# Another instruction list for the first three token blocks of a retention-and-MLP kernel, with named PSUM banks

## The chip, the cores and the metric

The kernel runs on one core of a Trainium2 chip. The metric is the device time of one execution in microseconds; of several runs the median is given. Five engines work side by side, each through its own queue in order: PE (matrix multiplications), DVE, ACT and POOL (element-wise work, copies, conversions) and SP, which here only issues DMAs. POOL and ACT issue some DMAs as well.

## The reference

Retention for 8 batches of 8 heads, 576 tokens and 64 channels, then one MLP with a sine activation over all 4608 tokens:

```python
scores = scale * q @ k.T                        # per batch and head, scale = 1/8
ret    = scores * gamma[h] ** (i - j)           # where i >= j, else 0
x      = (ret @ v) -> [4608 tokens, 512]        # heads side by side
h      = x @ w_in                               # 512 -> 2048
g      = h + sin(alpha * h) ** 2 / (alpha + 1e-9)
out    = g @ w_out                              # 2048 -> 512
```

gamma[h] is 1 - 2^(-5-h). Inputs and output are float32; the kernel multiplies in float16.

## The kernel before, in words

**Tokens.** The first 512 tokens of each batch make a block of the MLP: block n (0 to 7) needs batch n. The last 64 tokens of all eight batches, the ends, make block 8. A batch's 512 tokens are two halves, p = 0 and 1, of two chunks each.

**Retention of a batch** (class Attention). `load` brings q, k or v of a half from DRAM, 512 KB, by SP, into one of six `raw` buffers. `cast` multiplies q and k with the decay factors and makes float16 (v only becomes float16). `turn` transposes on PE and `take` copies the result from PSUM; for batches 2 and later `crossed` transposes by DMA instead, issued by SP. `scores` multiplies k and q (L318), `masked` applies the causal mask on DVE and gives `ret` (L329). `outer` makes each chunk's k-times-v state (L266), `evict`, `take_sum`, `more`, `next_sum` and `to_state` carry it from chunk to chunk (POOL or DVE). `values` multiplies ret and v in two passes (L356), `add_states` adds the earlier state times q (L374), and `keep` copies the result to xT (float16), the input of the MLP.

**MLP of a block.** There are 16 slices of 128 hidden channels, fc 0 to 15. `project(n, fc)` is four matmuls into one PSUM bank (L486), `sine` on ACT (L494), `square` on ACT, DVE or POOL (L503, L505), `product` on DVE gives gT (L510). `gemm2(n, u)` is four matmuls of the output (L530): output tile c = u // 4 (128 tokens), and slices 4 (u % 4) to 4 (u % 4) + 3. `finish` copies a tile to SBUF and stores it. A projection and a unit of gemm2 are the same amount of PE work, four matmuls of 512 columns.

**Weights.** `load_w_in(g)` brings the columns of fc 4g to 4g + 3, `load_w_out(g)` the rows of the same slices; POOL issues them, and the DMA converts them to float16. `wait_for_w_out(g)` is a small DMA on SP that reads that group, so that what stands behind it in SP's queue is issued only when the group has arrived.

**The order.** Everything stands in a manual schedule: each engine executes its instructions in the order of the program text, and waits for what an instruction reads and for the release of the buffer that it writes. From L571 to L1024 the order of batches 0 to 3 and blocks 0 to 2 is one list written out. From L1026 a loop over blocks 3 to 8 places the work of batch n + 1, the loads and casts of batch n + 2 and the ends between the projections of block n and the units of gemm2 of block n - 1. `keep_busy` multiplies zeros.

**PSUM.** Eight banks: tag `hp` has three buffers of one bank, `op` one, `mm` two of two banks. Whoever asks for a buffer of a tag gets the one that comes free first.

## Time and profile before

| what | us |
|---|---|
| median of 3 runs | 319.76 (319.76 to 322.72) |
| profiled execution | 320.69 |
| its span | 318.9 |
| PE busy in the span | 301.3 (94%) |
| DVE, ACT, POOL busy | 216.9, 174.0, 137.3 |
| first projection starts | 19.9 |
| loop starts (first projection of block 3) | 115.5 |
| last block's units of gemm2 begin | 299.4 |

Times in the profile are from the span's start. A busy PE is not PE at its peak, and idle time of an engine that ends no wait costs nothing. L numbers are lines of the kernel before. A row of the timeline gives start, duration, engine, line, operation, output<-inputs and count; what stands in brackets is the idle time before and what ended it.

### The profile page before, as it was taken

The numbers are of one execution on the slowest core, as the hardware profiler recorded it, in microseconds if no ns is written. First come the engines' busy times: TensorE is split into PE (matmuls) and PEld (weight loads), VectorE is DVE, ScalarE is ACT, GpSimd is POOL, SyncE is SP. The second block draws the span as 40 slices with busy tenths as digits, with TensorE's granted clock in tenths as the row PEclk, the third lists the DMA queues.
The fourth block names the chain that finished last, engine by engine and source line by source line (L and its number), as shares of the span: only waits on it lengthen the run. The fifth ranks groups of instructions, "written<-read, shape, count | busy, mean of one in ns | idle before, by whom it ended". The sixth has DMA issues, their size and how long they took to land.

```text
span 318.9 us, 7711 instructions
## 1 busy us (share of the span) xinstructions
PE 301.3 (94%) x3180; PEld 143.9 (45%) x3180; DVE 216.9 (68%) x316; ACT 174.0 (55%) x269; POOL 137.3 (43%) x140
## 2 busy tenths in 40 slices
PE   7889999699799999999999999999999999999994
PEld 2554454244344444444444444444444444444442
DVE  2778877669468989687878787878746565655500
ACT  3548654498356645464547454745465565456411
POOL 0866542472866961993299329922720000000000
PEclk9999999799999999999999999999999999999999
DMA  8999999999994559996999589952352111111232
GB/s 211 266 202 209 299 242 280 218 239 232 213 248 144 84 113 251 262 171 134 245 255 184 123 240 257 155 113 67 72 82 49 35 35 33 36 33 34 57 77 66
DMA packets 103108, 49.96 MB, mean 157 GB/s; under 512 B 44944, under 2 KB 98592, under 8 KB 103072
## 3 DMA queue, kind: packets, MB, share of 16 engines
q1 hardware_dynamic: 98352, 45.12, 63.1%
q0 software_dynamic: 4224, 4.19, 8.0%
q8 instruction: 25, 0.41, 0.6%
q10 hardware_dynamic: 496, 0.15, 0.2%
q14 instruction: 11, 0.09, 0.1%
HBM read 36.85 MB, written 9.44 MB: 145 GB/s over the span
## 4 chain that ended last, share of the span: by engine, by line
PE 78%; DMA 9%; DVE 6%; ACT 2%; POOL 2%; issue 2%; ACTq 0%; POOLq 0%; DVEq 0%
PE hps L486 35%; PE ops L530 34%; DMA v<-in_v_dram 5%; DMA q<-in_q_dram 3%; PE sc L318 2%; PE o L356 2%; DVE gT L510 2%; DVE ret L329 2%; DVE ss_t L505 1%; DMA k<-in_k_dram 1%; PE kv L266 1%; ACT s_t L494 1%; PE o L374 1%; PE idle L543 1%; ACT ss_t L503 1%
## 5 line engine op out<-in xcount | busy, mean ns | idle before, releaser
L494 ACT ACTIVATE s_t<-hps,alpha_t 128x512 f16<-128x512 f32 x144 | 97.9, 685 | 97.1 <-PE hps L486 96.7
L530 PE MATMUL ops<-w_out,gT 128*128 128x512 f16 x580 | 144.0, 378 | 0.9 <-ACT osb L102 0.5
L510 DVE SCALAR_TENSOR_TENSOR gT<-ss_t,inva,hps 128x512 f16<-128x512 f16 x144 | 106.1, 746 | 49.4 <-ACT ss_t L503 42.1
L486 PE MATMUL hps<-xT,w_in 128*128 128x512 f16 (+1 forms) x520 | 129.3, 380 | 3.6 <-DVE xT L104 2.1
L486 PEld LDWEIGHTS <-w_in 128*128 128x128 f16 x584 | 56.8, 98 | 71.2 <-issue 5.9
L530 PEld LDWEIGHTS <-gT 128*128 128x128 f16 x580 | 54.3, 98 | 64.5 <-DVE gT L510 0.9
L505 DVE TENSOR_TENSOR ss_t<-s_t 128x512 f16<-128x512 f16 x88 | 54.0, 614 | 17.3 <-ACT s_t L494 17.2
L329 DVE TENSOR_TENSOR ret<-sc,mask 128x1024 f16<-128x1024 f32 x32 | 38.6, 1218 | 1.7 <-PE sc L318 1.6
L293 POOL TENSOR_TENSOR s<-kvs,cn 128x256 f16<-128x256 f32 x20 | 13.4, 670 | 49.4 <-ACT kvs L102 47.1
L161 POOL TENSOR_TENSOR k<-k,cn 128x1024 f16<-128x1024 f32 (+1 forms) x13 | 24.8, 1911 | 17.3 <-DMA k<-in_k_dram 17.3
L102 ACT COPY osb<-ops 128x512 f32<-128x512 f32 (+1 forms) x36 | 20.5, 573 | 16.8 <-PE ops L530 14.2
L503 ACT ACTIVATE ss_t<-s_t 128x512 f16<-128x512 f16 x45 | 28.3, 631 | 0.6
L161 POOL TENSOR_TENSOR q<-q,cn 128x1024 f16<-128x1024 f32 (+1 forms) x15 | 27.3, 1822 | 1.1 <-DMA q<-in_q_dram 1.0
L102 ACT CAST xT<-o 128x1024 f16<-128x1024 f32 (+1 forms) x16 | 13.6, 881 | 13.0 <-PE o L374 12.8
L505 POOL TENSOR_TENSOR ss_t<-s_t 128x512 f16<-128x512 f16 x11 | 11.3, 1039 | 13.4 <-ACT s_t L494 12.7
L486 PE MATMUL hps<-xS,w_in 128*128 128x512 f16 x64 | 16.4, 379 | 0.0
L104 POOL CAST v<-v 128x1024 f16<-128x1024 f32 (+1 forms) x12 | 13.0, 1084 | 6.5 <-DMA v<-in_v_dram 6.5
L301 POOL TENSOR_TENSOR kvs<-s,kvs 128x256 f32<-128x256 f32 x19 | 15.1, 792 | 1.5
L356 PE MATMUL o<-ret,v 64*64 64x128 f16 x512 | 13.0, 220 | 1.8 <-issue 0.6
L300 POOL TENSOR_TENSOR s<-kvs,cn 128x256 f32<-128x256 f32 x19 | 12.1, 635 | 2.8 <-ACT kvs L102 2.7
L318 PE MATMUL sc<-qT,kT 64*64 64x128 f16 x512 | 12.1, 220 | 0.7 <-DVE qT L104 0.4
L356 PEld LDWEIGHTS <-v 64*64 64x64 f16 x512 | 8.8, 106 | 7.9 <-issue 7.8
(52 smaller groups left out, 126.7 us busy)
## 6 DMA issues: line engine op xcount, KB each, us to landing
out_dram<-osb SPq DMA_DIRECT2D x70, 128.0 KB, 2.4
k<-in_k_dram SPq DMA_DIRECT2D x16, 512.0 KB, 6.7
q<-in_q_dram SPq DMA_DIRECT2D x16, 512.0 KB, 6.4
v<-in_v_dram SPq DMA_DIRECT2D x16, 512.0 KB, 7.1
w_in<-in_moe_w_in_dram POOLq DMA_DIRECT2D x4, 512.0 KB, 8.1
w_out<-in_moe_w_out_dram POOLq DMA_DIRECT2D x4, 512.0 KB, 10.0
ks<-in_k_dram SPq DMA_DIRECT2D x8, 128.0 KB, 5.8
qs<-in_q_dram SPq DMA_DIRECT2D x8, 128.0 KB, 3.8
```

What stands on the lines that cost most here:

```text
L102: eng.copy(d_, s_)
L161: eng.tensor_tensor(dst[:, a0:a1].rearrange("p a r t d -> p t (a r) d"), t_.rearrange("p (t a) x -> p t a x", t=2)[:, :, a0:a1].rearrange( ...
L301: nc.gpsimd.tensor_tensor(self.kvs[:, c], s32, self.kvs[:, c], ADD)
L318: matmul(sc[halves(g), t, c : c + 128], kT[halves(t), 2 * a + r, halves(g)], qT[halves(t), 2 * a : 2 * a + 2, halves(g)], start=(z == 0 an ...
L329: nc.vector.tensor_tensor(ret.rearrange("p t (z x) -> p (t z) x", z=2), sc.rearrange("p t (z x) -> p (t z) x", z=2), mask[:, 0:256].unsque ...
L356: matmul(o[t][halves(e), c : c + 128], v16[halves(g), 4 * t + 2 * x + e, r, :], self.ret[p, x][halves(g), t, m : m + 128], start=(not same ...
L486: matmul(hps_of[n, fc][0][:, cols], w_in16[:, a, fc * P : (fc + 1) * P], xs[n][:, a, cols], start=(a == 0 and part != 1), stop=(a == KT - ...
L494: nc.scalar.activation(s_t, hps, mybir.ActivationFunctionType.Sin, bias=0.0, scale=alpha_t[:, fc : fc + 1],)
L503: nc.scalar.activation(ss_t, s_t, mybir.ActivationFunctionType.Square)
L505: eng.tensor_tensor(ss_t, s_t, s_t, MULT)
L510: nc.vector.scalar_tensor_tensor(gT[n][:, fc, :], ss_t, inva[:, fc : fc + 1], hps, MULT, ADD)
L530: matmul(ops[n, c][:, cols], gT[n][:, fk, c * P : (c + 1) * P], w_out16[:, fk, cols], start=(fk == 0 and cols.start == 0), stop=(fk == FC ...
```

## The change

The list of L571 to L1024 is replaced by another one with the same operations, and the loop keeps its order. Every PSUM tile now names its bank: h0, h1, h2 and op (one bank each), m0 and m1 (two banks each), one buffer per name; in the loop h2, h0, h1 and m0, m1 go in turn. Of the list's 48 projections 14 are made in two halves of 256 columns (2 before). The ends are worked for all batches at once, and each group of four batches has its output in one pair of banks. A tile of the output is stored by one DMA instead of two, and the last tile is made in two column halves, each with its own bank; the second half is stored by ACT's queue.

The core of the diff, with the new list in the stretches that follow:

```diff
-            ops[n, c] = psum.tile([P, 512], F32, tag=tag, bufs=1 if tag == "op" else 3, name="ops")
+            ops[n, c, cols.start] = psum.tile([P, 512], F32, tag=tag, bufs=1, name="ops")
...
-        for h in range(2):
-            nc.sync.dma_start(rows_of(n, c, h)[:, cols], osb[halves(h), cols])
+        (issue or nc.sync).dma_start(rows_of(n, c)[:, :, cols], osb[:, cols])
...
+        keep_busy(2, "h0")
+        keep_busy(8, "op")
+        keep_busy(10, "op")
+        keep_busy(4, "op")
+        load(0, "q", 0)
+        cast(0, "q", 0, G_, (1,))
+        cast(0, "q", 0, V, (0,))
+        turn(0, "q", 0, "h0")
+        load(0, "k", 0)
+        cast(0, "k", 0, G_, (0,))
+        cast(0, "k", 0, V, (1,))
+        turn(0, "k", 0, "op")
+        take(0, "q", 0, A_)
+        take(0, "k", 0, V, (0,))
+        take(0, "k", 0, V, (1,))
+        load(0, "k", 1)
+        cast(0, "k", 1, G_)
+        load(0, "q", 1)
+        cast(0, "q", 1, V)
+        load_w_in(0)
+        turn(0, "k", 1, "h1")
...
+        cast(0, "v", 0, G_)
+        at[0].outer((0,), "op", "h0")
+        load_w_in(1)
+        at[0].take_sum(0, A_)
+        load(0, "v", 1)
+        cast(0, "v", 1, G_)
+        at[0].scores(1, 0, "m1")
+        at[0].outer((1,), "op", "h1")
...
+        at[0].to_state(2, G_)
+        load_w_in(2)
+        load(1, "q", 0)
...
+        project(0, 0, "m1", 0)
+        load(1, "k", 0)
+        at[0].keep(1, A_, V)
+        project(0, 0, "m1", 1)
...
+        project(0, 6, "h1")
...
+        load(1, "k", 1)
+        load(1, "q", 1)
+        load(1, "v", 0)
...
+        project(0, 10, "m0")
+        project(0, 9, "h2")
+        sine(0, 9)
+        cast(1, "k", 0, G_, (0,))
+        load_w_in(3)
+        load_w_out(0)
...
+        cast(1, "k", 1, G_)
+        load_w_out(1)
...
+        gemm2(0, 0, "h1")
...
+        gemm2(0, 1, "h1")
+        load(1, "v", 1)
+        load_w_out(2)
...
+        load(3, "k", 1)
+        load(2, "k", 0)
...
+        load_w_out(3)
...
+        cast(2, "k", 0, G_)
+        at[1].to_state(2, V)
+        cast(3, "k", 1, G_, (1,))
+        load(2, "v", 0)
+        load(2, "q", 0)
+        cast(2, "q", 0, G_)
+        cast(2, "v", 0, G_)
+        load(2, "k", 1)
+        cast(2, "k", 1, G_)
+        load(2, "q", 1)
+        cast(2, "q", 1, G_, (0,))
+        cast(2, "q", 1, G_, (1,))
+        load(3, "k", 0)
+        crossed(2, 0, "k")
+        cast(3, "k", 0, G_)
+        crossed(2, 0, "q")
+        load(2, "v", 1)
+        cast(2, "v", 1, G_)
...
+        at[1].keep(1, A_)
+        at[1].keep(0, V, A_)
+        crossed(2, 1, "k")
+        load(3, "q", 0)
+        crossed(2, 1, "q")
+        crossed(3, 0, "k")
+        load(3, "v", 1)
+        cast(3, "q", 0, G_, (1,))
+        cast(3, "q", 0, G_, (0,))
+        load(3, "q", 1)
+        crossed(3, 0, "q")
+        gemm2(0, 15, "op")
+        gemm2(0, 3, "h1")
+        project(1, 2, "m1")
+        load(3, "v", 0)
...
+        finish(0, 0)
...
+        at[2].to_state(2, G_)
+        cast(3, "v", 1, G_)
...
+        at[3].scores(0, 1, "m0")
...
             if n == 7:
...
+                at_unit(1, lambda: E[0].scores(next(m)), lambda: E[1].scores(next(m)))
...
+                at_unit(8, lambda: E[0].values(False, next(m)), lambda: E[1].values(False, next(m)))
...
+        for cols, issue in ((slice(0, 256), nc.sync), (slice(256, 512), nc.scalar)):
+            tag = next(h)
+            for u in range(12, 16):
+                gemm2(NBLK - 1, u, tag, cols)
+            finish(NBLK - 1, 3, cols=cols, issue=issue)
```

Of the engines' instructions in the whole kernel little changes in number: DVE makes 4 `next_sum` steps instead of 20, POOL 8 squares instead of 11, ACT 49 instead of 45, and PE 29 matmuls on zeros instead of 31.

## The prediction

> **What bounds the kernel now.** I read the stages first: busy time of each engine in seven stretches of the span (columns: stretch, length, PE, weight loads, DVE, ACT, POOL with their instruction counts, granted clock, DMA share, GB/s).

> ```profile
> 0.00:19.90 19.90, 15.50 (x281) 8.16 (x282) 11.52 (x20) 7.66 (x11) 10.56 (x17) 1.00 1.05 230
> 19.90:35.40 15.50, 15.50 (x80) 7.83 (x80) 11.76 (x23) 11.92 (x19) 6.41 (x8) 1.00 1.22 231
> 35.40:59.20 23.80, 19.39 (x308) 10.34 (x307) 19.32 (x31) 10.42 (x18) 12.86 (x10) 1.00 1.13 267
> 59.20:88.70 29.50, 26.54 (x306) 11.69 (x306) 19.49 (x28) 20.27 (x32) 16.67 (x17) 0.94 1.02 223
> 88.70:115.50 26.80, 26.19 (x317) 12.12 (x315) 22.03 (x28) 16.74 (x26) 21.01 (x21) 1.00 0.70 145
> 115.50:299.40 183.90, 183.30 (x1821) 86.94 (x1822) 131.81 (x188) 102.69 (x158) 69.80 (x72) 1.00 0.59 128
> 299.40:318.90 19.50, 14.88 (x73) 6.82 (x70) 1.02 (x2) 4.30 (x8) 0.00 (x0) 1.00 0.29 68
> ```

> PE is the bound. In the loop (115.5 to 299.4) it idles 0.6 us of 183.9, so the loop keeps its length; time can come only from the list before it and from the tail. The list has 2.96 + 4.41 + 0.61 us of idle PE after the first projection and, in its fourth stretch, a clock of 0.94. The PE timeline shows the largest hole and the slow matmuls behind it:

> ```profile
> 56.46 0.59 PE L486 MATMUL hps<-xT,w_in 128*128 128x512 f16 x2 [0.30 <-ACT xT L102]
> 59.17 7.46 PE L486 MATMUL hps<-xT,w_in 128*128 128x512 f16 x26 [2.12 <-DVE xT L104]
> ...
> 87.35 0.59 PE L374 MATMUL o<-qT,s 64*64 64x128 f16 x16 [1.30 <-POOL s L293]
> ```

> 26 matmuls took 7.46 us where the warm spacing of 0.216 us (four per 0.864 us throughout the chain) gives 5.6: 1.9 us lost after a gap of 2.12 us.

> In the same stretches the DMA share is above 1, so I asked in which order the DMA serves its queues. These are the queues in single microseconds (packets, MB, share): 12 to 13, then 14 to 15, then 20 to 21.

> ```profile
> q1 hardware_dynamic: 567, 0.29, 116.7%
> ...
> q0 software_dynamic: 203, 0.21, 124.3%
> ...
> q0 software_dynamic: 203, 0.21, 124.1%
> ```

> w_in(0) was issued by POOL at 10.11, yet until 13 only the k/q/v loads move, and then weights alone: whoever was issued first is served first. From the packet rates, a load (1024 packets at 575 per us) takes 1.78 us and a weight group (528 at 205) 2.57; data are usable some 1.3 us after.

> **Accounting.** PE work between the first projection (19.9) and the loop: 80 units (48 projections, 32 output units) of 0.864 us = 69.1; attention 3.9 a batch (a loop block lasts 31.57 in the chain, 141.16 to 172.73, less 32 units = 27.65), three batches 11.8; batch 1's four transposes by PE at 0.45, 1.8. Sum 82.7. The stretch lasts 95.6, so 12.9 is lost: 7.98 idle, 1.9 clock, 3.0 small change at switches and restarts.

> **Part 1, the start.** Loads come in the same rhythm with q ahead of k (data at 5.0, 7.1, 9.0, 10.8, 12.4, 14.4; the waits of the DVE casts and the issue rows). The 24 matmuls on zeros in front end at about 8.2 (9 at 0.43 us, 15 at 0.216), before anything on PE could run, as both casts of k end at 8.3. Then: both turns to 9.1, k1 cast by POOL 9.05 to 11.0 (1.9), turned to 11.45; v1 cast by POOL 14.4 to 15.6 behind the issue of w_in(1); outer, two scores, two masks at 1.2, values, states, keep at 1.0. The first projection starts at 20.2 to 21.0: I take 20.6, **0.7 later**.

> **Part 2, weights.** POOL issues w_in(0) at 11.0 and w_in(1) at 13.7 behind its casts, and batch 1's loads no longer wait for w_out(0) (the gate was issued at 25.5). In order of issue, with about two loads standing in the SP queue, the DMA serves: q of batch 1 to 15.2, w_in(0) 17.8, k 19.6, w_in(1) 22.2 (usable 23.4), two loads 25.8, w_in(2) 28.4, w_in(3) 31.0, w_out(0) 33.5, two loads 37.1, w_out(1) 39.7 (usable 41.0). PE wants w_in(1) at 22.0 for fc 6, its second projection: 1.4 of wait. It then wants w_in(2) at 29.0, usable 29.7, and w_out(1) at 40.1: 0.7 and 0.9. Sum **3.0**; 0 if weights overtake the loads, 5.4 if they share with them (below). Between 37 and 41 PE also waits for products (ACT has 0.685 + 0.63 for a sine with its square, DVE 0.746 for each product): 1.4.

> **Part 3, the rest of the list.** Followed in order with these rows (product 0.69 back to back, mask 1.2, DVE square 0.42, POOL cast 1.9), PE starts block 1 at 54 and reaches the loop with only 1.1 us of further waits. What goes: the gap at 56 to 59, with it the 1.9 of clock (DVE's cast of batch 2's q stood before the copy of batch 1's xT and waited for its load until 56.56; now POOL makes every cast of batch 2), and the wait for POOL's state at 87 (POOL had waited for v until 82.25; batch 2's v is now loaded by about 60). The cover: POOL converts batch 2 and most of 3 in one row of 16.9 us, about 52 to 69; the scores of batch 2 come at 68 and 74, its transposes land near 62 and 69. The scores of batch 3 come at 82, their last transpose at 75 to 80. Two additions. Restarts and switches as before, 3.0. And DVE squares beside POOL:

> ```profile
> L505 DVE TENSOR_TENSOR ss_t<-s_t x88: 414/425/2130, 22.8 to 298.5; 128x512 f16<-128x512 f16 x88
> ```

> The median is 0.425, but some beside a POOL cast take up to 2.13; four of block 1's DVE squares fall into POOL's row, so 0 to 6.8 on a DVE that is about 87% full (48 of 55 us by its rows); 1.0 of it reaches PE, near the median. Lost in the middle: 3.0 + 1.4 + 1.1 + 3.0 + 1.0 = 9.5 against 12.9: **3.4 gained**.

> **Part 4, ends and loop.** Same matmuls, masks and copies; the loop idles 0.6 us in all: 0, with -0.3 to +0.5 for a DVE that enters the loop with some 2 us of arrears. One store DMA in place of two lies under the loop: 0.

> **Part 5, the tail.**

> ```profile
> 313.77 0.37 ACT L102 COPY osb<-ops 128x256 f32<-128x256 f32 x1 [2.48 <-PE ops L530]
> 314.19 0.60 PE L530 MATMUL ops<-w_out,gT 128*128 128x256 f16 x4 [0.50 <-ACT osb L102]
> 314.87 0.37 ACT L102 COPY osb<-ops 128x256 f32<-128x256 f32 x1 [0.73 <-PE ops L530]
> ```

> The second half's matmuls wait for the copy of the first, as both are one bank, and four DMAs then go out on SP, the last issued by 316.55. With a bank for each half PE ends near 314.1, the copy at 314.6, and one issue on ACT (0.39 to 0.48 at the start of the run) is over by 315.05, 1.5 earlier. A store of 128 KB instead of 64 KB (2.4 against 2.0 to landing) gives back up to 0.4. I take **1.3** (0.5 to 1.5).

> **Sum.** -0.7 + 3.4 + 1.3 = 4.0 gained. The profiled execution took 320.69 us (span 318.9 and 1.8 around it): 316.7. It stood 0.93 above the median of the runs, 319.76; against that, **315.7**.

> **Rivals.**
> A. Weights overtake and the list runs as tightly as the stretch 88.7 to 115.5 did (0.61 idle): the 3.0 of weights and the 1.0 of squares go: 311.7. For it: w_out(3), issued at 39.10, was served ahead of a v load issued at 38.87. Against: that load's issue ended only at 40.48.
> B. No difference that counts: weights and loads share, or squares and casts hold DVE up by 3 more; then only the tail and a little remain: 318.4. Sharing as a mechanism here: each weight group takes 2 x 2.57 while loads stand in the queue, w_in(1) is usable at 25.8, PE idles 3.8 and runs at half clock for 3.2 us (as from 59.4 to 62.6), 1.6: 5.4 instead of 3.0, so 318.1. For it: at 31 to 32 both queues moved (79.4% and 39.9%). Against: 13.6 to 29 was weights alone, though that had no load behind it until 26.2.
> [...]
> C. Slower: SP's in-order queue. Ahead of the scores of batch 3 stand six loads and six transposes, from 54 on. At the rows of a full DMA six transposes of 3.5 to issue and five loads of 1.9 are 30.5 us, from 54.5 to 85; the last of them lands 7.2 after its issue began, near 89: PE stands 7 us at 82, and 1.6 of clock follow: 324.3. It decides from a landing after 82, and makes the kernel 1% slower than before from 88. For it: transposes from 54.78 to 90.58 were issued at those rates. Against: by bytes six of each take about 23 us, to 78.
> **Chances.** Forecast 0.5 (its own spread 313 to 318.5, a quarter of it within 1%), A 0.15, B 0.22 (0.08 of it by sharing), C 0.13. 1% is 3.2 us, about what a measurement of this kernel tells from no change. Faster: 0.37 + 0.15 + 0.03 of B = 0.55; same 0.13 + 0.18 = 0.31; slower 0.14. The range 311 to 321 leaves out half of A's lower side and C.

> **What would show it.** First projection near 20.6 and a PE wait of about 1.4 before the second; weights and loads taking turns in whole pieces; no gap over 2 us at 54 to 60 and a clock of 1.00 there; loop from about 113; in the tail no PE wait for the copy and the last issue near 1.5 after PE's end at most. Wrong if kT or qT of batches 2 or 3 release PE, if PE stands over 2 us for w_in, or if DVE squares of 1 to 2 us line up before PE waits for gT.

## The result and the profile after

The changed kernel takes 374.96 us (median of four runs, 374.3 to 377.88) beside 320.24 for the kernel before: a ratio of 1.171, 95% interval 1.162 to 1.180. It is 17% **slower**, where 315.7 was forecast, and lies far outside the range.

First the profile page of the changed kernel: busy time by engine, then the span in 40 slices (tenths of busy time of PE, granted clock, DMA share), then the group of the scores' matmuls.

```profile
PE 310.2 (82%) x3238; PEld 154.7 (41%) x3238; DVE 218.9 (58%) x303; ACT 171.2 (46%) x269; POOL 141.7 (38%) x151
...
PE   8679899999669679969992599809998999999920
...
PEclk9969999999969699989998699967999999999985
DMA  8999998959597898596665975669237110111111
...
L319 PE MATMUL sc<-qT,kT 64*64 64x128 f16 x512 | 14.0, 248 | 37.2 <-DMA qT<-q 30.4
```

PE has 3238 matmuls instead of 3180, since more projections and the last tile are made in halves; their work is the same but for two matmuls on zeros. It is now idle for 65.9 us of the 376.1, most of it in five holes from 94 us on (the slices of 9.4 us with 0, 2, 5, 6 and 7 from the eleventh on) and at the end, and the clock sinks with each hole (to 6 to 8 tenths in the slices of the holes or just behind them). The scores (L319) wait for qT, which a DMA transposes. The prediction had named this as a sign of being wrong ("if kT or qT of batches 2 or 3 release PE").

The same by stretches, columns as in the table of stretches above. The first fence is the changed kernel. The second is the changed list with two stores for each tile, the first experiment below.

```profile
0.00:40.00 40.00, 32.91 (x380) 18.66 (x381) 25.81 (x41) 18.20 (x30) 21.80 (x27) 0.91 1.12 246
40.00:80.00 40.00, 37.48 (x505) 20.27 (x503) 33.44 (x41) 24.56 (x41) 27.87 (x28) 1.00 1.02 222
80.00:100.00 20.00, 19.81 (x285) 10.51 (x283) 13.23 (x17) 11.72 (x18) 10.96 (x14) 1.00 0.66 62
100.00:120.00 20.00, 13.26 (x166) 6.86 (x165) 10.87 (x13) 7.49 (x12) 9.88 (x10) 0.83 0.86 198
...
200.00:220.00 20.00, 9.36 (x123) 4.62 (x125) 7.18 (x10) 4.01 (x8) 4.26 (x5) 0.74 0.78 119
...
360.00:376.10 16.10, 0.00 (x0) 0.00 (x0) 0.00 (x0) 0.00 (x0) 0.00 (x0) 0.61 0.12 45
```

```profile
0.00:40.00 40.00, 33.64 (x394) 20.09 (x395) 26.59 (x44) 19.92 (x33) 23.99 (x29) 0.91 1.11 241
40.00:80.00 40.00, 37.74 (x508) 19.97 (x509) 34.52 (x40) 24.40 (x40) 27.68 (x28) 1.00 1.10 243
80.00:100.00 20.00, 19.81 (x314) 10.75 (x311) 15.35 (x21) 11.78 (x18) 12.72 (x16) 1.00 0.99 229
100.00:120.00 20.00, 19.35 (x268) 9.80 (x267) 17.52 (x24) 13.01 (x21) 10.44 (x11) 1.00 0.70 138
...
200.00:220.00 20.00, 20.00 (x198) 9.46 (x197) 15.77 (x23) 11.02 (x17) 8.40 (x11) 1.00 0.40 86
```

Up to 80 us the two are alike: the list as such does not stall. From 80 on the DMA shares of the changed kernel look ordinary (0.66, 0.86, 0.78), but the bytes do not always go with them: from 80 to 100 us it moves 62 GB/s at a share of 0.66, where the second kernel moves 229 at 0.99. The last 16 us hold no engine's work at all, only DMA, at a share of 0.12.

SP's issues show what happens at 75 us. First the changed kernel, then the list with two stores (start, duration, what is issued):

```profile
75.80 10.26 SPq L521 DMA_DIRECT2D out_dram<-osb  x4
86.15 8.39 SPq L185 DMA_TRANSPOSE kT<-k  x1
...
97.45 2.38 SPq L114 DMA_DIRECT2D q<-in_q_dram  x1
99.94 4.17 SPq L185 DMA_TRANSPOSE qT<-q  x1
```

```profile
74.44 5.77 SPq L522 DMA_DIRECT2D out_dram<-osb  x8
80.30 1.31 SPq L185 DMA_TRANSPOSE kT<-k  x1
...
82.94 0.56 SPq L114 DMA_DIRECT2D q<-in_q_dram  x1
83.61 2.92 SPq L185 DMA_TRANSPOSE qT<-q  x1
```

Both send the four tiles of block 0 there. With one DMA a tile, the four issues take 10.26 us and the transpose behind them 8.39; with two, the eight issues take 5.77 and the transpose 1.31. The q load behind them is issued 14.5 us later (97.45 against 82.94), the transpose of q 16.3 us later (99.94 against 83.61), and the last scores of batch 3 wait for that transpose at 107; scores of the batches after it wait like this in the loop, for up to 10.80 us:

```profile
106.91 1.07 PE L319 MATMUL sc<-qT,kT 64*64 64x128 f16 x32 [6.64 <-DMA qT<-q]
```

The tail, which was forecast to gain, in the timelines of ACT and of its queue:

```profile
359.48 0.37 ACT L103 COPY osb<-ops 128x256 f32<-128x256 f32 x1 [1.37 <-PE ops L528]
359.89 1.13 ACTq L521 DMA_DIRECT2D out_dram<-osb  x1
```

The copy no longer waits behind the other half and the issue follows it at once, as forecast; but the span ends at 376.1, 16.2 us after the copy. Before it ended 3.7 us after it.

### The profile page after: what moved, and what is told of

It is laid out like the page before. It is cut to its first block, busy times and chain, and to the rows that moved or that the text cites. A ratio compares the mean times of both kernels' runs of the same rounds, so it can differ in the third digit from the quotient of the medians.

```text
span 376.1 us, 7784 instructions
## 1 busy us (share of the span) xinstructions
PE 310.2 (82%) x3238; PEld 154.7 (41%) x3238; DVE 218.9 (58%) x303; ACT 171.2 (46%) x269; POOL 141.7 (38%) x151
## 4 chain that ended last, share of the span: by engine, by line
PE 39%; DMA 20%; SPq 15%; issue 9%; POOL 7%; DVE 3%; ACT 3%; POOLq 0%; ACTq 0%; DVEq 0%
PE ops L528 19%; PE hps L486 17%; DMA v<-in_v_dram 6%; SPq L114 5%; SPq L185 5%; DMA qs<-in_q_dram 4%; SPq L121 3%; DMA w_in<-in_moe_w_in_dram 3%; DMA k<-in_k_dram 3%; DMA qT<-q 2%; ACT s_t L494 2%; DMA qTs<-qs 2%; DVE gT L510 1%; PE sc L319 1%; DMA ks<-in_k_dram 1%
## 5 line engine op out<-in xcount | busy, mean ns | idle before, releaser
L528 PE MATMUL ops<-w_out,gT 128*128 128x512 f16 (+1 forms) x592 | 149.5, 385 | 1.0 <-DMA w_out<-in_moe_w_out_dram 0.9
L486 PE MATMUL hps<-xT,w_in 128*128 128x512 f16 (+1 forms) x568 | 132.1, 369 | 2.0 <-DVE gT L510 1.0
L486 PEld LDWEIGHTS <-w_in 128*128 128x128 f16 x632 | 62.9, 100 | 70.3 <-issue 9.6
L528 PEld LDWEIGHTS <-gT 128*128 128x128 f16 x592 | 56.9, 100 | 66.1 <-issue 7.9
L505 DVE TENSOR_TENSOR ss_t<-s_t 128x512 f16<-128x512 f16 x87 | 51.0, 586 | 37.4 <-ACT s_t L494 36.9
L319 PE MATMUL sc<-qT,kT 64*64 64x128 f16 x512 | 14.0, 248 | 37.2 <-DMA qT<-q 30.4
L162 POOL TENSOR_TENSOR k<-k,cn 128x1024 f16<-128x1024 f32 (+1 forms) x17 | 29.5, 1736 | 18.9 <-DMA k<-in_k_dram 18.9
L503 ACT ACTIVATE ss_t<-s_t 128x512 f16<-128x512 f16 x49 | 30.8, 633 | 0.8 <-DVE gT L510 0.3
L162 POOL TENSOR_TENSOR q<-q,cn 128x512 f16<-128x512 f32 (+1 forms) x16 | 25.2, 1579 | 14.4 <-DMA q<-in_q_dram 14.4
L319 PEld LDWEIGHTS <-kT 64*64 64x64 f16 x512 | 10.2, 124 | 44.8 <-issue 35.6
L103 ACT COPY osb<-ops 128x512 f32<-128x512 f32 (+1 forms) x34 | 19.5, 574 | 15.5 <-PE ops L528 12.9
L103 ACT CAST xT<-o 128x1024 f16<-128x1024 f32 (+1 forms) x14 | 12.9, 954 | 9.5 <-PE o L375 8.9
L486 PE MATMUL hps<-xS,w_in 128*128 128x512 f16 x64 | 16.4, 379 | 0.0
L105 POOL CAST v<-v 128x1024 f16<-128x1024 f32 (+1 forms) x15 | 15.2, 1016 | 2.9 <-DMA v<-in_v_dram 2.8
L505 POOL TENSOR_TENSOR ss_t<-s_t 128x512 f16<-128x512 f16 x8 | 9.3, 1164 | 17.9 <-ACT s_t L494 17.6
L301 POOL TENSOR_TENSOR s<-kvs,cn 128x256 f32<-128x256 f32 x23 | 14.5, 631 | 3.6 <-ACT kvs L103 3.3
```

What stands on the lines that cost most here:

```text
L103: eng.copy(d_, s_)
L162: eng.tensor_tensor(dst[:, a0:a1].rearrange("p a r t d -> p t (a r) d"), t_.rearrange("p (t a) x -> p t a x", t=2)[:, :, a0:a1].rearrange( ...
L319: matmul(sc[halves(g), t, c : c + 128], kT[halves(t), 2 * a + r, halves(g)], qT[halves(t), 2 * a : 2 * a + 2, halves(g)], start=(z == 0 an ...
L486: matmul(hps_of[n, fc][0][:, cols], w_in16[:, a, fc * P : (fc + 1) * P], xs[n][:, a, cols], start=(a == 0 and part != 1), stop=(a == KT - ...
L503: nc.scalar.activation(ss_t, s_t, mybir.ActivationFunctionType.Square)
L505: eng.tensor_tensor(ss_t, s_t, s_t, MULT)
```

## The experiments

**My theory** after this comparison: `finish` hands one DMA a pattern of 2 x 64 rows x 512, and such a DMA is carried by 2 of the 16 DMA engines only (2/16 = 0.125, the share in the tail), at some 50 GB/s (the rate from 362 to 372 us), or 5.2 us for 256 KB. Everything that passes through the same two engines behind it, a share of each load and transpose, lands late. **Rivals:** the new list itself (too many loads and transposes in SP's queue, rival C); or stores of 256 KB, or half as many of them, whatever their pattern.

### The changed list with two stores for each tile

```diff
-        (issue or nc.sync).dma_start(rows_of(n, c)[:, :, cols], osb[:, cols])
+        for h in range(2):
+            (issue or nc.sync).dma_start(rows_of(n, c)[h, :, cols], osb[halves(h), cols])
```

> The changed kernel, but each tile (and each half of the last) is stored by two DMAs of 64 rows again. Theory S (a store written as 2 x 64 x 512 runs on 2 of the 16 DMA engines: with it the DMA share stands at 0.13 and about 50 GB/s while nothing else moves, after PE's end): the whole loss goes, 313 to 319 us, the loop without waits of PE for transposes, the stores landing in 2 to 4 us. Rival L (the new list or its banks starve PE by themselves): it stays above 340.

Measured: 315.17 us (314.88 to 315.85), ratio to before 0.984 (0.981 to 0.988). The whole loss is in the store, and the rest of the change lands within 0.6 us of the 315.7 forecast. Its PE waits, in full down to 1.0 us:

```profile
PE tr L195 <- POOL k L162: 1.8, 2, 1.6
PE hps L486 <- DVE gT L510: 1.4, 3, 0.7
PE idle L542 <- DVE zero L568: 1.2, 1, 1.2
PE o L375 <- issue: 1.2, 1, 1.2
PE ops L529 <- DMA w_out<-in_moe_w_out_dram: 1.0, 1, 1.0
```

No transposed tile is among them, nor among the shorter ones but for a copy of qT by DVE (0.2 us). Rival C falls.

### The kernel before with one store for each tile

```diff
-        for h in range(2):
-            nc.sync.dma_start(rows_of(n, c, h)[:, cols], osb[halves(h), cols])
+        nc.sync.dma_start(rows_of(n, c)[:, :, cols], osb[:, cols])
```

`rows_of` gives the whole tile's pattern here, as in the change.

> The kernel before with one change: each tile is stored by one DMA of 2 x 64 x 512. S: slow as the changed kernel is, 350 to 385 us, with PE waiting for transposes and loads in the loop and 10 us or more between the last copy and the end of the span. L: no change within 1%, 317 to 323.

Measured: 376.7 us (375.57 to 377.53), ratio 1.176 (1.170 to 1.181). The one line costs the old list 56 us and the new one 60, so it is no property of the new order. The old list waits for the same thing (list of PE's waits: total, times, longest):

```profile
PE sc L318 <- DMA qT<-q: 33.0, 7, 10.1
```

### The kernel before with only the tail changed

```diff
-        for cols in (slice(0, 256), slice(256, 512)):
-            gemm2(NBLK - 1, 15, "hp", cols)
-            finish(NBLK - 1, 3, cols=cols)
+        for cols, issue in ((slice(0, 256), nc.sync), (slice(256, 512), nc.scalar)):
+            for u in range(12, 16):
+                gemm2(NBLK - 1, u, "hp", cols)
+            finish(NBLK - 1, 3, cols=cols, issue=issue)
```

with a bank for each half, and two stores each.

> The kernel before with the last tile in two halves of their own banks, the second half issued by ACT, two DMAs for each half. If the wait of the second half's matmuls for the copy of the first is worth what the tail showed: 0.5 to 1.5 us faster, 318.3 to 319.3 where the kernel before has 319.8. If the store sets the end alone: no difference.

Measured: 319.7 us (317.28 to 321.09), ratio 0.9968 (0.9938 to 0.9998): 1.0 us, the interval from 0.1 to 2.0, which holds the forecast 1.3 and only just leaves out zero. The copy of the second half starts at 313.40 instead of 314.87 and the issue takes 1.19 us on ACT's queue.

### The kernel before with one store for each tile of block 8 only

```diff
+        if n == 8:
+            nc.sync.dma_start(rows_of(n, c)[:, :, cols], osb[:, cols])
+            return
```

> The kernel before, but the four tiles of the last block alone are stored by one DMA each. S: PE ends as before near 314, the last store lands 12 to 16 us after the last copy instead of 3.7, 330 to 334 us. M (the loss comes from DMAs and waits in the loop, not from the single store): 319 to 321.

Measured: 330.18 us (329.71 to 330.65), ratio 1.031 (1.024 to 1.038). Nothing follows these stores, so this is their own price: 14.0 us from the last copy to the end of the span instead of 3.7. A two-microsecond window of that stretch:

```profile
320.00:322.00 2.00, 0.00 (x0) 0.00 (x0) 0.00 (x0) 0.00 (x0) 0.00 (x0) 0.50 0.13 50
```

DMA share 0.13, 50 GB/s, and no engine at work. The packet records of the changed kernel, whose last tiles are stored in the same pattern, say the same: from 355 to 362 us rows of 2048 bytes are in flight two at a time (four for 0.34 us in all), a new pair every 80 ns; in the tail of the kernel before up to 16 are (17 for 5 ns). Tiles of block 8 come every 3.45 us (the spacing of its copies in the changed kernel) and each needs 5.2 us at this rate, so they pile up.

### Two stores of 128 KB for each tile, cut by columns

```diff
-        (issue or nc.sync).dma_start(rows_of(n, c)[:, :, cols], osb[:, cols])
+        half_cols = (cols.stop - cols.start) // 2
+        for c0 in (cols.start, cols.start + half_cols):
+            part = slice(c0, c0 + half_cols)
+            (issue or nc.sync).dma_start(rows_of(n, c)[:, :, part], osb[:, part])
```

> Edit: the changed kernel, but each tile goes out in two DMAs by columns (2x64x256 each, 128 KB), not by rows: as many DMAs, as large, as in the kernel before. Theory (the split over engines follows the slowest dimension, which is still 2): both run on two engines, about 375, 365 to 390, with a DMA share of 0.13 after PE's last matmul. Rival (size or number of the DMAs is what counts): 314 to 318, as with two stores by rows.

Measured: 380.0 us (379.89 to 380.11), ratio 1.183 (1.175 to 1.192). As many stores as in the kernel before, with as many bytes, and as slow as one of 256 KB; the tail again shows a share of 0.14 with no engine at work. Size and number are out. What the fast stores lack and these two slow forms share is the outermost dimension of 2. A share of 0.14 of 16 engines is 2.2 engines, here at 44 to 48 GB/s.

### One store of 256 KB for each tile, of 128 whole rows

The converse. The pattern has the dimension of 2 because a tile's rows stand in the order even, odd; here the projection reads them back into row order (blocks 0 to 7; block 8 keeps two stores):

```diff
+            x = xs[n][:, a, cols]
+            if n < 8:
+                x = x.rearrange("p (c h i) -> p c i h", h=2, i=64)
...
+        if n < 8:
+            r0 = 576 * n + 128 * c
+            (issue or nc.sync).dma_start(out[r0 : r0 + 128, cols], osb[:, cols])
+            return
```

> Edit: the changed kernel, but the tokens of blocks 0 to 7 are put back into row order where the projection reads them (its moving operand is read with a stride of 64 elements between the pairs), so that a tile of 128x512 goes out as one DMA of 128 rows, whole rows in order; block 8 keeps two DMAs of 64 rows for each tile. The number of stores of blocks 0 to 7, and their 256 KB, are those of the changed kernel; the split of the DMA is not. [...] Rival (one DMA of 256 KB is too large, or half as many DMAs disturb the order of the queue): 360 to 380 as in the changed kernel, with waits for qT and kT of 10 us each.

Measured: 445.57 us (445.39 to 445.97), ratio 1.388 (1.381 to 1.395). By my theory of the store this run had to come near the 315.17 of the list with two stores. The total went the wrong way, and for a reason of its own: the strided operand (groups of PE by shape, mean ns after the busy time).

```profile
L489 PE MATMUL hps<-xT,w_in 128*128 128x512 f16 x456 | 236.0, 645 | 0.2 <-DMA w_in<-in_moe_w_in_dram 0.2
...
L489 PE MATMUL hps<-xS,w_in 128*128 128x512 f16 x64 | 16.4, 379 | 0.0
```

A matmul of a projection from xT now has a mean of 645 ns, one from xS, still read in order, 379 as ever. The records of the matmuls from xT, with those of 256 columns, add up to 265.3 us (236.0 + 29.3) instead of 129.9 (114.7 + 15.2) in the list with two stores: 135 us more, about the whole difference between the two times (130). The question of the stores is answered by their own row (median us to landing last), and PE waits for no transpose:

```profile
out_dram<-osb SPq DMA_DIRECT2D x32, 256.0 KB, 2.3
```

Since a slower PE gives the DMA more time, the same was done without that cost: the copies that write xT bring the tokens into row order, and the projection reads without a stride.

```diff
-                    self.x[:, :, cols].rearrange("p (t x) n -> p t x n", t=2),
-                    self.both[p].rearrange("p t (x n) -> p t x n", x=2),
+                    self.x[:, :, cols].rearrange("p y (c i h) -> p y c h i", i=64, h=2),
+                    self.both[p].rearrange("p t (x c h i) -> p (t x) c h i", x=2, c=2, h=2),
...
```

The copies of one bank are changed alike, and the store is that of the run before.

> Edit: the list, with blocks 0 to 7 brought into row order by the copies that write xT (two-byte elements written 4 bytes apart), so that the projection reads them without a stride and each tile of these blocks goes out in one DMA of 128 whole rows; block 8 keeps two DMAs of 64 rows. The store of 256 KB is as large, and the stores as many, as in the changed kernel; PE is not slowed by its operand as in the run before. Theory (only the split over the engines counts): each store lands in 2 to 3 us, no wait for qT or kT of 10 us, 315 as with two stores, 314 to 317, or up to 1 us more where the strided copies are slower (0.59 us each now). Rival (size or number of the stores): 340 and more.

Measured: 316.06 us (315.64 to 317.27), ratio 0.987 (0.982 to 0.991). One store of 256 KB lands in 2.3 us and does no harm. Against the list with two stores it loses 0.9 us, which the intervals do not separate; ACT's copies to xT became dearer (16.5 us for 14 of them instead of 12.9). The store's pattern, not its size and not the number of stores, is the cause.

### The kernel before with only the new ends

```diff
-                for w, E in enumerate((Ends(0), Ends(2))):
-                    at_unit(5 * w, lambda E=E: E.scores())
...
+                E = (Ends(0), Ends(2))
+                at_unit(1, lambda: E[0].scores(), lambda: E[1].scores())
+                behind(1, E[0].masked)
+                behind(2, E[1].masked)
+                at_unit(8, lambda: E[0].values(False), lambda: E[1].values(False))
+                at_unit(8, lambda: E[0].values(True), lambda: E[1].values(True))
+                at_unit(8, E[0].add_states, E[1].add_states)
+                for i in range(4):
+                    at_unit(9 + i, lambda i=i: E[i // 2].keep(i % 2, A_))
```

Each group of four batches has its output in one pair of banks, as in the change.

> Edit: the kernel before with only the ends of all batches in one bank pair at a time (block 7's units 1, 2, 8 and 9 to 12 in place of 0, 4, 5 and 9). The prediction costs this part at 0: 319.5 to 321, ratio 0.997 to 1.003. Rivals: two drains of PE fewer give 0.3 to 0.6 (ratio 0.998); the four copies by ScalarE, spread over four units, make a product late: plus 0.5 to 1 us.

Measured: 320.37 us (319.68 to 321.61), ratio 0.9983 (0.9954 to 1.0012): no difference, as forecast.

### The list with two stores and PE kept busy at the start

In the list with two stores the granted clock is 0.50 from 17.7 to 24.5 us (the windows 17 to 18 and 24 to 26 have 0.84 and 0.87), up into the first projections. PE is busy for 7.65 of the 12 us from 8 to 20 there, which is 64% and not the 70% of the expectation below. Three matmuls on zeros more before the second outer products, three more before the first values, five before the first states:

```diff
+        keep_busy(3, "h2")
         at[0].outer((1,), "op", "h1")
...
-        keep_busy(1, "h2")
+        keep_busy(4, "h2")
         at[0].values(0, False, "m0")
...
+        keep_busy(5, "h2")
         at[0].add_states(0)
```

> Edit: the list with two stores for each tile (315.2 before this run), and matmuls on zeros put into the stretch from 15 to 20.5 us: three before the second outer products, four in place of one before the first values, five before the first states are added. In the list with two stores PE is busy for 70% of 8 to 20 us and the granted clock is 0.50 from 17.8 to 24.3 us; before, it was busy for 80% there and the clock stayed 1.00. Theory (idle time of PE sets the clock back even where no gap is longer than 1.6 us): the clock stays 1.00 through 24 us and the time falls by 1.3 to 2.5 us, to 312.7 to 313.9. Rival (the clock falls for another reason): still 0.50 there, and 315 to 316, the fillers at half clock taking some tenths.

Measured: 315.81 us (315.2 to 316.31), ratio 0.983 (0.979 to 0.988). No gain. The clock held until 20.66. A stretch of 1.45 us without PE, from 18.89 to 20.34, in which its queue waited for nothing that the trace shows, came before; the five fillers took 2.27 us at half clock; the first projection moved from 22.54 to 24.44. Without those five (the edit against the run just told):

```diff
-        keep_busy(5, "h2")
```

> Edit: the list with two stores and the first two of the three fillers (three matmuls on zeros before the second outer products, four in place of one before the first values), without the five before the first states, which took 2.27 us at half clock in the run with three fillers and moved the first projection from 22.5 to 24.4 us. Theory: the clock stays 1.00 until about 20.7 us as in that run, the states are added at 20.6 as without fillers, the first projection starts at 22.0 to 22.5 and the half-clock stretch is no longer than without fillers: 313.5 to 315.3, ratio 0.979 to 0.985. Rival (the half-clock stretch has a length of its own of 3.4 to 6.5 us wherever it begins): it then lies under the projections from 20.7 to 24.5 or later, and nothing is gained: 315 to 317.

Measured: 314.76 us (314.16 to 315.13), ratio 0.981 (0.977 to 0.985). The clock of the profiled execution is 1.00 up to PE's end, and yet only 0.4 us are gained on the 315.17, which the intervals do not separate from nothing. PE's timeline shows why:

```profile
21.84 1.12 PE L486 MATMUL hps<-xT,w_in 128*128 128x256 f16 x8 [0.15 <-ACT xT L103]
24.00 8.83 PE L486 MATMUL hps<-xT,w_in 128*128 128x512 f16 x48 [1.04 <-DMA w_in<-in_moe_w_in_dram]
```

The first projection is done sooner and then the second stands until 24.00 for its weights. In the list with two stores it starts at 24.22: the half clock had covered that wait, and 1.04 us of what the faster clock gave came back as a wait for w_in. Of the six executions two have a mean clock of 1.00 (314.16 and 314.39) and four one of 0.991 to 0.995 (314.68 to 315.13), so the fillers do not always hold the clock. This version has the lowest median, 1.9% below the kernel before.

## Why the prediction was wrong

**The step that failed** is in part 4: "One store DMA in place of two lies under the loop: 0." It was put at nothing without a row for a DMA of this pattern, and how such a DMA is carried was not asked. It costs 60 us: 374.96 against 315.17. By the two spans (376.1 and 313.1, 63.0 apart), 12.6 of it are the longer tail (16.2 us instead of 3.6 behind the last copy), 39.3 more idle time of PE ahead of that (65.9 idle in all against 14.1, less the tail), and 11.1 more busy time of the same matmuls, since the granted clock falls to 0.74 to 0.91 in the stretches with holes. Part 5's "up to 0.4" for a store of 128 KB instead of 64 KB failed with it: the bound came from rows of DMAs of 64 rows, while the pattern of the new one has no row in the trace of before. Such an operation called for a wide bound, and I gave it none.

That two engines carry such a store is read from its share: 2 of 16 make 0.125, and the share is 0.13 for the 2x64x512 store, with two rows in flight at a time, and 0.14 for its halves by columns. Stores with other outermost dimensions than 2, 64 and 128 were not tried, and which two engines carry it, no view here shows.

What such a store does to other DMAs can be read from the changed kernel's packets. The v load issued at 110.35 stands right behind two stores. Of its 1024 rows of 512 bytes 896 start between 114.4 and 117.9 us, while the stores run, and the other 128 only between 121.8 and 123.4, after the last row of the stores (121.76). These are the packets between 512 bytes and 2 KB in the two windows, 912 - 16 and 140 - 12:

```profile
DMA packets 1000, 0.66 MB, mean 188 GB/s; under 512 B 16, under 2 KB 912, under 8 KB 998
DMA packets 140, 0.07 MB, mean 42 GB/s; under 512 B 12, under 2 KB 140, under 8 KB 140
```

128 of 1024 is 2 of 16, which fits the theory: the part of the load that falls to the two engines waits for the stores, and the rest does not. A transpose loses more than its eighth. Of the 1024 rows of the one issued at 86.15, 469 start by 92.1; 19 of these then stand in flight for 7.5 to 8.6 us, and the other 555 start from 99.41 on, right behind the last row of block 0's stores (99.36). Rows that stand count as busy, which is why the share of 80 to 100 us looks ordinary: 0.47 of the 0.66 is these 19. SP's issue adds to it, 8.39 us for that transpose instead of 1.31, so what follows is also issued late. How the waits of the scores divide between the two is not shown.

**Rival C** had the right place and sign, late transposes behind SP's queue, scores waiting for them, a clock that falls, but the wrong mechanism: by its own six loads and six transposes the list does not stall, as the two stores show.

**The other steps** are read in the list with two stores, whose profile answers to the forecast:

- *Start.* Forecast 20.6 for the first projection, 22.54 measured. 1.2 us of PE's "issue" idle time before the states were not foreseen, and half clock stretched the rest. At full clock, in the last experiment, it is 21.84. So the term of -0.7 measured -2.64.
- *Weights.* By order of issue w_in(1) was to be usable at 23.4; PE got it at 24.0 in the last experiment, where its wait of 1.4 was 1.04. In the list with two stores it cost nothing, as half clock covered it, and w_in(2), at 0.7, cost nothing either; w_out(1) was to cost 0.9, and 0.96 was measured (PE's wait until 42.03). The mechanism behind these dates was only partly right. These are the queues at 17 to 18 us in the list with two stores:

```profile
q0 software_dynamic: 138, 0.14, 82.8%
q1 hardware_dynamic: 141, 0.07, 35.2%
```

  Weights and loads move together, 138 and 141 packets, as in the rival of sharing. But the weights get 70% of the time (82.8 of 118.0) and not the half that this rival takes, which may be why the dates came out near. Up to 15 us, w_in(0) being issued at 11.15, only the loads move, as by order of issue.
- *Middle.* From the first projection to the loop 88.3 us (22.54 to 110.85) instead of 95.6: the gain of 3.4 measured 7.3. The hole at 56 to 59 is gone, as forecast (block 1 starts at 55.0, 54 forecast), the clock is 1.00 from 55 on, and PE idles 1.73 us between there and the loop. Of the 9.5 us to be lost, 5.6 were, 3.1 of it idle time; the term for squares beside POOL (their maximum is 2.07 us, 2.13 before) and the 1.4 for products together show as 1.4 of waits for gT.
- *Ends and loop.* 0 forecast, a ratio of 0.9983 measured alone; the loop from 110.85 to 295 idles 0.56 us.
- *Tail.* 1.3 forecast, 1.0 measured alone. The wait for the copy went as forecast, but the one issue on ACT's queue, put at 0.39 to 0.48, took 1.13 in the changed kernel.

The sum of 4.0 came out as 5.8 on the spans (318.9 to 313.1) and 5.7 on the medians beside each other, from a start 1.9 worse and a middle 3.9 better than forecast. That it lies so near the forecast is partly two errors that offset each other.

## What to carry to other kernels

When a change merges DMAs, write down the merged pattern's dimensions first: a tile of 128 partitions stored as 2x64 rows moved at 50 GB/s, which makes 5.2 us, while the same 256 KB as 128 rows landed in 2.3 us. In a profile this shows as a DMA share that stands at a small part of 16 while nothing else moves (0.13 here, 2 of 16), as few bytes for the share where other DMAs stand behind it (62 GB/s at 0.66), and as late transposes and loads far from the store. If the tile's rows are interleaved, either keep one DMA for each half or restore the order in a copy that is made anyway, and not in PE's operand.
